# Attention's value and memory products on the full 128x128 array, and other prices in the list schedule

## The chip, the cores and the metric

The kernel runs as one program on one core of a Trainium2 chip. TensorE (PE) does the matmuls, VectorE (DVE) and ScalarE (ACT) the elementwise work, GpSimd (POOL) a few memsets, and SyncE (SP) issues all the DMAs. The metric is the device time of one execution in microseconds; lower is better.

## The reference

Attention with a memory, and then two feed-forward layers over the tokens that it gives:

```python
B, H, S, D = 4, 8, 576, 64            # batches, heads, tokens, head width
scores = q @ k.T / sqrt(D)            # causal
local = softmax(scores) @ v
q_p = phi(q)                          # phi(x) = max(x, 0) + min(exp(x), 1)
mem_out = (q_p @ M_prev) / (q_p @ z_prev + 1e-6)
x = g * mem_out + (1 - g) * local     # g = sigmoid(beta), by head
# 2304 tokens, d_model 512, d_ff 2048
h = x @ w_in;   x = (s * relu(h) ** 2 + b) @ w_out
h = x @ w_in2;  out = (max(h, 0) + alpha * min(h, 0)) @ w_out2
```

## The kernel before, in words

Attention works head by head, and the memory part by pair of heads. A head's 576 queries stand in five chunks of 64, 128, 128, 128 and 128, and a chunk sees the keys up to its last query, so 64, 192, 320, 448 and 576 of them. Chunks 0 to 2 are set 0, chunks 3 and 4 are set 1; a set's results gather in one PSUM bank. For each chunk `scores` makes the scores in one of the banks for scores (`sp`, two of them after the first batch) and their exponentials, `turn` splits the normalised weights in two float16 parts and transposes them by a DMA (L564), and `products` (L584) multiplies them with the values, 128 keys at a time, into the bank `ob`. Every chunk's number of keys ends in half a block: the last product of each chunk reads 64 keys, so 64 rows of the array.

`features` (L454, L463) computes the memory part of a pair with queries on the partitions. `remembered` (L598) turns it with a matmul against the identity into the bank `ob`, on top of what the products give. Batches 0 and 1 do this by pair (`pair`, with float32 scores, L627). Batches 2 and 3 do it head by head (`head`, with float32r scores, L673 and L674): each head turns its own 64 columns, and then ACT (L695) takes one half of the bank's rows and DVE (L697) adds the other half. The array's tile is as large as the operands: 64 key rows give a tile of 64 rows, 64 output rows one of 64 columns. The profile writes it as 64\*128 (rows \* columns).

The feed-forward layers (called MoE in the code) run over blocks of tokens, and over 16 slices of d_ff in each: 12 matmuls for the first product (L800 to L802) and 12 for the second (L834 to L836) a slice. Layer 1 has blocks of 512, 320 and 320 tokens and then four of 288, layer 2 eight of 288. Blocks 0 to 2 lie in batches 0 and 1, blocks 3 and 4 in batch 2, blocks 5 and 6 in batch 3 (block 0 needs only batch 0). A batch's attention goes to DRAM (`x1`, L719) and a block is read from it (L890).

The order on every engine is fixed when the program is built. `Plan.order` is a list schedule: each operation has a duration and a priority, attention's coming before the layers', and an engine takes the most urgent of what its own clock says is ready. On the chip an engine then keeps that order and waits on semaphores. So prices such as `t_r` (a float32r matmul) and the rate of a DMA (transposes are those with a `dur` of 500 or more) decide the order alone:

```python
dma_free = max(dma_free + (110.0 if dur < 500 else 30.0), t + min(dur, 625.0) + 650.0) + nbytes / (360.0 if dur < 500 else 290.0)
def t_r(n):
    return max(108.0, n / 2.4 + 2.5)
```

Of the kernel before, what the change touches and what calls it, by code (L numbers as in the profile page):

```python
# [18 lines left out]
# tokens of the blocks of the two layers: (first, tokens); layer 1's first takes both places of the operands  # L19
# [6 lines left out]
# query chunks: (first query, queries); a chunk sees the keys up to its last query  # L26
CHUNKS = [(0, 64), (64, 128), (192, 128), (320, 128), (448, 128)]
SETS = [(0, 1, 2), (3, 4)]
# chunks whose weights are transposed together
# [16 lines left out]
FLEX = 'x'  # L46
# [7 lines left out]
class Slot:  # L54
    """A tenant of the pool of equal slots; it gets its place when the operations are ordered."""
# [6 lines left out]
class Plan:  # L62
    """Operations in a logical order with what they read and write. order() is a list schedule
    of the graph: every engine takes, of the operations that are ready, the most urgent. A slot
    is taken by its first operation, if as many more are free as the slot's reserve asks, and
    is free again after its last."""
# [38 lines left out]
    def either(self, ways, **kw):  # L105
        """An operation for whichever of the engines comes to it first: ways is {engine: (duration, function)}."""
        eng = next(iter(ways))
        i = self.op(eng, *ways[eng], **kw)
        if len(ways) > 1:
            self.ways[i] = ways  # L110

    def order(self):
# [32 lines left out]
        def spot(t, s):  # L145
            """Where a slot could go: the last extra place, or else the one that has been free for longest."""
# [12 lines left out]
        while len(out) < n:  # L159
# [50 lines left out]
            if e == "PE":  # L210
                # at half the clock unless the last tick was busy enough
                todo, now, k = dur, t, int(t / TICK)
                while todo > 0:
                    rate = 1.0 if busy.get(k - 1, 0.0) >= WARM else 0.5
                    step = min(todo, max(0.0, (k + 1) * TICK - now) * rate)
                    busy[k] = busy.get(k, 0.0) + step
                    todo -= step
                    now += step / rate
                    k += 1
                dur = now - t  # L220
            free[e] = t + dur
            done[i] = t + dur
            if nbytes:
                dma_free = max(dma_free + (110.0 if dur < 500 else 30.0), t + min(dur, 625.0) + 650.0) + nbytes / (360.0 if dur < 500 else 290.0)
# [25 lines left out]
def t_r(n):  # L250
    return max(108.0, n / 2.4 + 2.5)
# [18 lines left out]
def build(tc, kd, kz, qd, vd, qp, mzd, beta8, sb2, win1, wout1, win2, wout2, alpha, outT):  # L270
# [7 lines left out]
    with tc.tile_pool(name="sb", bufs=1) as sb, tc.tile_pool(  # L278
# [5 lines left out]
        # the parts of a slice of d_ff: w_in's and w_out's; before they are there, the last slices' room serves as slots  # L284
# [13 lines left out]
        def cut(t, n, k, step=None):  # L298
            """The first n elements of the k-th part of t."""
# [28 lines left out]
        def at(s, n, dt=F32):  # L328
            """The first n elements of a slot, as dt."""
# [12 lines left out]
        # the last 128 columns: -8e9 where the key lies after the query  # L342
# [7 lines left out]
        def consts():  # L350
            # wsc = (1 + exp(beta)) / LIFT = 1 / ((1 - g) LIFT); bgc = 1 + exp(-beta) = 1 / g
# [16 lines left out]
        # the banks of MoE products serve the first batch's attention  # L368
# [8 lines left out]
        def gate(hg, ahead, ahead0):  # L377
            """A load for a head waits for the scores of an earlier one."""
# [3 lines left out]
        def either(kind, a_dur, a_fn, d_dur, d_fn, **kw):  # L382
            """An operation for the scalar or, of the kinds in FLEX, also for the vector engine."""
# [10 lines left out]
        # They are scaled by LIFT over the sum of their magnitudes, so that no part leaves float16's range.  # L394
        def values(b, p):
# [19 lines left out]
            # un = 1 / (scale LIFT)  # L415
# [53 lines left out]
        def scores(b, h, g, keys, scored):  # L469
            """keys: what the products read; scored: (rows, columns) -> the product's instructions."""  # L470
# [4 lines left out]
            for c in cs:  # L475
# [4 lines left out]
                # keys in one or two banks: (bank, column of maximum and sum, first key, keys)  # L480
# [10 lines left out]
                for bk, col, k0, kn in parts_s:  # L491
                    sp = bank_of[bk][0:nq, 0:kn]
                    dur, mm = scored(sp, q0, nq, k0, kn)
# [20 lines left out]
            # rows 64.. of chunk 0's column were set once and stay finite  # L514
# [8 lines left out]
        def turn(b, g, group, parts, turned):  # L523
            """group: what is transposed together, (head of the pair, chunk)."""
# [13 lines left out]
            for pw, c in group:  # L538
# [19 lines left out]
                # what is transposed with the chunk's last 64 keys has to be something; nothing uses it  # L558
# [8 lines left out]
        def products(g, part, parts, turned, sf, obk, ok, high, rows, first=False):  # L567
            """The products with the values: part (head of the pair, chunk) into rows of the bank. high: the high and
            low parts of the values go to the same rows, else the low ones follow in the next 64."""
# [6 lines left out]
            def mm():  # L576
                P = p_t()
                W = at(sf, 2 * NKB * 2 * D, FP16).rearrange("p (n h e) -> p n h e", h=2, e=2 * D)
                for kb in range(nkb):
                    kk = min(128, nk - kb * 128)  # L580
                    cols = [(slice(0, D), kb), (slice(D, 2 * D), kb), (slice(0, D), nkb + kb)] if high else [
                        (slice(0, 2 * D), kb), (slice(0, 2 * D), nkb + kb)]
                    for w, x in cols:
                        T.matmul(obk[rows, q0 - o0:q0 - o0 + nq], W[0:kk, kb, pw, w], P[0:kk, x, 0:nq],  # L584
# [4 lines left out]
        def remembered(g, heads, sa, obk, ok, rows, ch, first=True):  # L589
            """The memory part, transposed into the bank."""  # L590
# [3 lines left out]
            def mm():  # L594
                for c in cs:
                    q0, nq = CHUNKS[c]
                    F = at(sa, 2 * D * NC).rearrange("p (c e) -> p c e", c=NC)[0:nq, c, heads]
                    T.matmul(obk[rows, q0 - o0:q0 - o0 + nq], F, ident[0:nq, 0:nq], start=(first and c == cs[0]), stop=False,  # L598
                             skip_group_check=True)

            op("PE", sum(t_f(CHUNKS[c][1]) for c in cs), mm, r=[(sa, g), "ident"], w=[ok], prio=ATT + ch * 10)
# [7 lines left out]
        def pair(b, p, sqp, sa, sf, xt):  # L609
# [9 lines left out]
            for g, cs in enumerate(SETS):  # L619
# [4 lines left out]
                for odd in range(2):  # L624
                    def scored(sp, q0, nq, k0, kn, s=sk[odd]):
                        def mm():
                            T.matmul(sp, at(sqp, S)[:, q0:q0 + nq], at(s, S)[:, k0:k0 + kn], start=True, stop=True)  # L627
# [10 lines left out]
                remembered(g, slice(0, 2 * D), sa, obk, ok, slice(0, 128), ch0)  # L638
# [8 lines left out]
                # local + memory, transposed  # L647
# [7 lines left out]
        def head(b, h, sa, sf, xt):  # L655
# [15 lines left out]
            def scored(sp, q0, nq, k0, kn):  # L671
                def mm():
                    T.matmul(sp, qh[:, q0:q0 + nq], ks[:, k0:k0 + kn], start=True, stop=False)  # L673
                    T.matmul(sp, ql[:, q0:q0 + nq], ks[:, k0:k0 + kn], start=False, stop=True)  # L674
# [3 lines left out]
            for g, cs in enumerate(SETS):  # L678
# [9 lines left out]
                remembered(g, slice(D * odd, D * odd + D), sa, obk, ok, slice(r0, r0 + 64), ch0, False)  # L688
# [5 lines left out]
                # local + memory, transposed  # L694
                op("ACT", t_act(qn, 50, 93), lambda xr=xr, qn=qn, obk=obk: A.activation(  # L695
# [305 lines left out]
```

## Time and profile before

| | us |
|---|---|
| three runs | 1095.52, 1096.52, 1099.56 (median 1096.52) |
| profiled execution: its time (the listed one that fits the span) and its span | 1099.56, 1099.4 |
| PE busy | 1073.4, 98% of the span |
| DVE, ACT busy | 684.6 (62%), 529.8 (48%) |
| attention's last store of a batch to DRAM, batches 1, 2, 3 | issued at 246.71, 412.96, 568.99 |
| first feed-forward matmul | 104.85 |

Busy time of PE counts a matmul from start to end, and matmuls overlap in the pipeline. What a matmul costs is therefore read as the distance from its start to the start of the next, which the timeline gives.

### The profile page before, as it was taken

To read this page: it belongs to the slowest core of one execution; us is meant where nothing else is said; L and a number is where in the kernel's file an instruction comes from. 1 tells how busy PE (TensorE), PEld (TensorE's weight loads), DVE (VectorE), ACT (ScalarE), POOL (GpSimd) and SP (SyncE) were. 2 spreads that over 40 slices of the span, in tenths; PEclk is the share of its full clock that TensorE was granted. 3 is DMA by queue.
4 is the path that set the end of the run, shared out by engine and by line. 5 is a ranking of instruction groups with operands and counts; after the bars stand their busy time and mean duration, and the time that the engine had idled before them with its cause. 6 is when DMAs were issued, how large, how long until landed. Compare 5 with 4: busy or idle time off the path is not lost.

```text
span 1099.4 us, 20528 instructions
## 1 busy us (share of the span) xinstructions
PE 1073.4 (98%) x7776; PEld 976.4 (89%) x7776; DVE 684.6 (62%) x1812; ACT 529.8 (48%) x1325; POOL 32.2 (3%) x171
## 2 busy tenths in 40 slices
PE   7978999999999999999999999999999999999998
PEld 5755777777889989989999999999999999999998
DVE  6768888867575566566646179984545454545443
ACT  7764666558576667668654466331212121212111
POOL 1100000000000000000000000000000000000000
PEclk9987999999999999999999999999999999999999
DMA  8899686665644564454434055321101010100000
GB/s 211 162 182 259 203 182 192 181 141 167 134 72 125 132 135 109 118 125 106 96 105 154 1 185 193 129 73 32 44 1 44 1 44 1 44 1 22 1 22 23
DMA packets 163860, 114.10 MB, mean 104 GB/s; under 512 B 127408, under 2 KB 141744, under 8 KB 163760
## 3 DMA queue, kind: packets, MB, share of 16 engines
q1 hardware_dynamic: 163760, 112.78, 39.1%
q8 instruction: 61, 1.00, 0.4%
q14 instruction: 39, 0.32, 0.1%
HBM read 68.19 MB, written 14.16 MB: 75 GB/s over the span
## 4 chain that ended last, share of the span: by engine, by line
PE 88%; DMA 5%; DVE 2%; issue 2%; ACT 2%; SPq 0%; POOL 0%; DVEq 0%; POOLq 0%; ACTq 0%
PE yb L834 12%; PE yb L836 12%; PE yb L835 12%; PE hb L800 8%; PE hb L802 7%; PE hb L801 7%; PE ob L584 7%; PE sp L800 3%; PE sp L801 3%; PE sp L802 3%; PE ob L598 2%; PE sp L627 2%; DMA pool<-pool 2%; PE ob L802 2%; PE ob L800 2%
## 5 line engine op out<-in xcount | busy, mean ns | idle before, releaser
L834 PE MATMUL yb<-gr,wt 128*128 128x288 f32 (+3 forms) x960 | 299.0, 311 | 0.9 <-ACT gr L822 0.9
L835 PE MATMUL yb<-gr,wt 128*128 128x288 f32 (+3 forms) x960 | 291.7, 304 | 0.0
L836 PE MATMUL yb<-gr,wt 128*128 128x288 f32 (+3 forms) x960 | 291.6, 304 | 0.0
L822 ACT CAST gr<-gt 128x288 fp32r<-128x288 f32 (+2 forms) x240 | 107.4, 447 | 305.4 <-DVE gt L820 297.0
L823 DVE TENSOR_TENSOR gr<-gt,gr 128x288 fp32r<-128x288 f32 (+2 forms) x240 | 114.2, 476 | 139.1 <-ACT gr L822 138.6
L800 PE MATMUL hb<-xr,wt 128*128 128x288 f32 (+2 forms) x576 | 186.1, 323 | 1.7 <-ACT gt L814 1.7
L834 PEld LDWEIGHTS yb<-gr,wt 128*128 128x128 f32 x960 | 181.0, 189 | 7.6 <-issue 2.1
L836 PEld LDWEIGHTS yb<-gr,wt 128*128 128x128 f32 x960 | 181.3, 189 | 3.6 <-DVE gr L823 0.8
L835 PEld LDWEIGHTS yb<-gr,wt 128*128 128x128 f32 x960 | 180.9, 188 | 2.0 <-issue 0.2
L802 PE MATMUL hb<-xr,wt 128*128 128x288 f32 (+2 forms) x576 | 178.6, 310 | 0.0
L801 PE MATMUL hb<-xr,wt 128*128 128x288 f32 (+2 forms) x576 | 178.6, 310 | 0.0
L800 PEld LDWEIGHTS hb<-xr,wt 128*128 128x128 f32 x576 | 108.8, 189 | 8.6 <-ACT gt L814 2.6
L801 PEld LDWEIGHTS hb<-xr,wt 128*128 128x128 f32 x576 | 109.0, 189 | 2.9 <-issue 0.6
L802 PEld LDWEIGHTS hb<-xr,wt 128*128 128x128 f32 x576 | 108.9, 189 | 3.0
L814 ACT ACTIVATE gt<-hb 128x288 f32<-128x288 f32 (+2 forms) x112 | 49.7, 444 | 106.8 <-PE hb L802 105.8
L505 ACT ACTIVATE pool<-sp,mx 64x64 f32<-64x64 f32 (+2 forms) x153 | 72.4, 474 | 35.4 <-DVE mx L497 27.2
L584 PEld LDWEIGHTS <-pool 64*64 64x64 f16 (+3 forms) x930 | 55.1, 103 | 38.1 <-issue 19.7
L497 DVE CUSTOM_DVE_ANT_0 sp<-sp,mask 64x64 f32<-64x64 f32 (+4 forms) x132 | 56.5, 438 | 42.6 <-PE sp L674 26.5
L584 PE MATMUL ob<-pool 128*128 128x128 f16 (+5 forms) x855 | 76.8, 221 | 4.1 <-DMA pool<-pool 4.0
L800 PE MATMUL sp<-xr,wt 128*128 128x288 f32 x256 | 75.5, 295 | 0.0
L801 PE MATMUL sp<-xr,wt 128*128 128x288 f32 x256 | 75.5, 295 | 0.0
L802 PE MATMUL sp<-xr,wt 128*128 128x288 f32 x256 | 75.4, 295 | 0.0
(174 smaller groups left out, 1694.1 us busy)
## 6 DMA issues: line engine op xcount, KB each, us to landing
pool<-win SPq DMA_DIRECT2D x19, 512.0 KB, 4.4
pool<-wout SPq DMA_DIRECT2D x17, 512.0 KB, 4.5
room<-wout SPq DMA_DIRECT2D x15, 512.0 KB, 4.3
room<-win SPq DMA_DIRECT2D x13, 512.0 KB, 4.3
pool<-qd SPq DMA_DIRECT2D x16, 288.0 KB, 3.1
pool<-kd SPq DMA_DIRECT2D x16, 288.0 KB, 3.7
pool<-y SPq DMA_DIRECT2D x16, 288.0 KB, 3.4
out_t<-pool SPq DMA_DIRECT2D x32, 144.0 KB, 1.8
```

The source lines that it names most:

```text
L497: op("DVE", t_dve(kn, 1.04, 0 if mk is None else 60), lambda sp=sp, nq=nq, mo=mo, kn=kn, mcol=mcol, last=last: V.tensor_tensor_reduce(out= ...
L505: op("ACT", t_act(kn, 50, 180), lambda sp=sp, p_c=p_c, k0=k0, kn=kn, mcol=mcol, scol=scol: A.activation(out=p_c()[:, k0:k0 + kn], in_=sp, ...
L584: T.matmul(obk[rows, q0 - o0:q0 - o0 + nq], W[0:kk, kb, pw, w], P[0:kk, x, 0:nq], start=(first and kb == x == 0), stop=False, skip_group_c ...
L800: T.matmul(H_, W_h, X_h, start=(d == 0), stop=False)
L801: T.matmul(H_, W_h, X_l, start=False, stop=False)
L802: T.matmul(H_, W_l, X_h, start=False, stop=(d == KD - 1))
L814: op("ACT", t_act(n, 50), lambda: A.activation(out=t_, in_=H_, func=AF.Relu), r=[hk, "gr"], w=[tk], prio=-1)
L822: op("ACT", t_act(n), lambda: A.copy(out=G_h, in_=t_), r=[tk], w=[("gh", gj)], prio=-1)
L823: op("DVE", t_dve(n), lambda: V.tensor_tensor(out=G_l, in0=t_, in1=G_h.bitcast(F32), op=ALU.subtract), r=[tk, ("gh", gj)], w=[("gl", gj)], ...
L834: T.matmul(Y, W_h, G_h, start=(f == 0), stop=False)
L835: T.matmul(Y, W_l, G_h, start=False, stop=False)
L836: T.matmul(Y, W_h, G_l, start=False, stop=(f == KF - 1))
```

## The change

In batches 2 and 3 the memory part is turned once a pair (`recall`, new) in a score bank, all 128 columns at a time, and ACT or DVE writes it scaled to the output slot before the heads come. `head` no longer calls `remembered`; DVE adds both halves of its bank to the slot, one after the other, and ACT does none. In all batches `products` reads 128 rows of weights and values (the weights behind a chunk's last key were set to zero by POOL before the transpose), and the scores of chunk 0 and the turned memory part use 128 columns of the array; rows that nobody asked for are not read. Float32r matmuls, transposes and loads have other prices in the schedule. Comments are left out of the new file, and line numbers move: L673/L674 become L687/L688, L697 becomes L709, L800 to L802 L813 to L815, L834 to L836 L847 to L849; L584 and L598 stay.

```diff
-                dma_free = max(dma_free + (110.0 if dur < 500 else 30.0), t + min(dur, 625.0) + 650.0) + nbytes / (360.0 if dur < 500 else 290.0)
+                dma_free = max(dma_free + (110.0 if dur < 500 else 30.0), t + min(dur, 625.0) + 650.0) + nbytes / (330.0 if dur < 500 else 160.0)
...
 def t_r(n):
-    return max(108.0, n / 2.4 + 2.5)
+    return max(112.0, n * 0.4427 + 3.2)
...
                 for kb in range(nkb):
-                    kk = min(128, nk - kb * 128)
...
-                        T.matmul(obk[rows, q0 - o0:q0 - o0 + nq], W[0:kk, kb, pw, w], P[0:kk, x, 0:nq],
+                        T.matmul(obk[rows, q0 - o0:q0 - o0 + nq], W[:, kb, pw, w], P[:, x, 0:nq],
                                  start=(first and kb == x == 0), stop=False, skip_group_check=True)
...
-        def remembered(g, heads, sa, obk, ok, rows, ch, first=True):
+        def remembered(g, sa, obk, ok, prio):
...
-                    F = at(sa, 2 * D * NC).rearrange("p (c e) -> p c e", c=NC)[0:nq, c, heads]
-                    T.matmul(obk[rows, q0 - o0:q0 - o0 + nq], F, ident[0:nq, 0:nq], start=(first and c == cs[0]), stop=False,
+                    F = at(sa, 2 * D * NC).rearrange("p (c e) -> p c e", c=NC)[:, c]
+                    T.matmul(obk[:, q0 - o0:q0 - o0 + nq], F, ident[:, 0:nq], start=(c == cs[0]), stop=False,
                              skip_group_check=True)
...
+        def recall(b, p, sa, xt):
+
+            j = p % 2
+            for g in range(len(SETS)):
+                ok = next_bank(b, "S")
+                obk = bank_of[ok]
+                remembered(g, sa, obk, ok, ATT + cnt["ch"] * 10 - 4)
+                o0, qn = span_of(g)
+                either("x", t_act(qn, 50, 93), lambda o0=o0, qn=qn, obk=obk: A.activation(
+                    out=at(xt, S)[:, o0:o0 + qn], in_=obk[:, 0:qn], func=AF.Copy, scale=vsc[:, j, 1:2]),
...
+                    r=[ok, ("un", j)], w=[(xt, odd, g) for odd in range(2)])
...
-                    T.matmul(sp, qh[:, q0:q0 + nq], ks[:, k0:k0 + kn], start=True, stop=False)
-                    T.matmul(sp, ql[:, q0:q0 + nq], ks[:, k0:k0 + kn], start=False, stop=True)
+                    T.matmul(sp, qh[:, q0:q0 + 128], ks[:, k0:k0 + kn], start=True, stop=False)
+                    T.matmul(sp, ql[:, q0:q0 + 128], ks[:, k0:k0 + kn], start=False, stop=True)
...
-                remembered(g, slice(D * odd, D * odd + D), sa, obk, ok, slice(r0, r0 + 64), ch0, False)
...
-                op("ACT", t_act(qn, 50, 93), lambda xr=xr, qn=qn, obk=obk: A.activation(
-                    out=xr(), in_=obk[r1:r1 + 64, 0:qn], func=AF.Copy, scale=un[r0:r0 + 64]), r=[ok, ("un", j)], w=[(xt, odd, g)])
-                op("DVE", t_dve(qn, 1.04, 60), lambda xr=xr, qn=qn, obk=obk: V.scalar_tensor_tensor(
-                    out=xr(), in0=obk[r0:r0 + 64, 0:qn], scalar=un[r0:r0 + 64], in1=xr(),
-                    op0=ALU.mult, op1=ALU.add), r=[("un", j)], w=[ok, (xt, odd, g)])
+                for r, w in ((r1, []), (r0, [ok])):
+                    op("DVE", t_dve(qn, 1.04, 60), lambda xr=xr, qn=qn, obk=obk, r=r: V.scalar_tensor_tensor(
+                        out=xr(), in0=obk[r:r + 64, 0:qn], scalar=un[r0:r0 + 64], in1=xr(),
+                        op0=ALU.mult, op1=ALU.add), r=[ok, ("un", j)], w=w + [(xt, odd, g)])
...
-                    head(b, 2 * p, sa, sf, xt)
-                    head(b, 2 * p + 1, sa, sf, xt)
+                    recall(b, p, sa, xt)
+                    head(b, 2 * p, sf, xt)
+                    head(b, 2 * p + 1, sf, xt)
```

The order on PE before, in batch 2 at the end of the set 0 of a head: products, the memory part of this head (output 64 rows), then feed-forward matmuls.

```order
L584 MATMUL ob<-pool 128x128
L598 MATMUL ob<-ident,pool 64x64
L598 MATMUL ob<-ident,pool 64x128 x2
L834 MATMUL yb_93<-gr,wt_1750 128x322
L835 MATMUL yb_93<-gr,wt_1750 128x322
```

The same memory part in the changed kernel, now for both heads of the pair, in a score bank and between feed-forward matmuls:

```order
L815 MATMUL hb<-xr,wt_1825 128x320
L598 MATMUL sp_98<-ident,pool 128x64
L598 MATMUL sp_98<-ident,pool 128x128 x2
L813 MATMUL hb<-xr,wt_1825 128x320
L814 MATMUL hb<-xr,wt_1825 128x320
```

It has left the end of each head's set, stands once a pair before the heads' products, and its tile has 128 columns. In the whole program the array's tile changes its size 469 times from one matmul to the next before, 345 of them after the first feed-forward matmul and 233 after the first score of batch 2; in the changed kernel 108, 64 and 0 times.

The second place is where PE turns to the feed-forward layers for the first time. Before, score and product matmuls of batch 1 stand ahead of it:

```order
L627 MATMUL sp_98<-pool 128x288
L584 LDWEIGHTS pool
L584 MATMUL ob<-pool 64x64
L584 LDWEIGHTS pool
L584 MATMUL ob<-pool 64x64
L800 MATMUL hb<-xr,wt_885 128x512
L801 MATMUL hb<-xr,wt_885 128x512
```

In the changed kernel:

```order
L627 MATMUL sp_98<-pool 128x320
L627 MATMUL sp_99<-pool 128x192
L813 MATMUL hb<-xr,wt_982 128x512
L814 MATMUL hb<-xr,wt_982 128x512
L815 MATMUL hb<-xr,wt_982 128x512
L627 MATMUL sp_99<-pool 128x64
L627 MATMUL sp_98<-pool 128x192
```

The first 21 products of batch 1 and 8 of its score matmuls now come behind the first feed-forward matmul; 464 matmuls stand ahead of it in place of 493. From there on the two orders mix alike: when the last product of batch 1 stands, 342 feed-forward matmuls are ahead of it before and 357 after, and at the last product of batch 3 1791 and 1782.

## Rows read from the trace of the kernel before

**Rows 1.** Page, busy time by engine; granted clock of PE in 40 slices

```profile
PE 1073.4 (98%) x7776; PEld 976.4 (89%) x7776; DVE 684.6 (62%) x1812; ACT 529.8 (48%) x1325; POOL 32.2 (3%) x171
PEclk9987999999999999999999999999999999999999
```

**Rows 2.** Stages: length, then busy PE, PEld, DVE, ACT, POOL; clock, DMA share, GB/s

```profile
0.00:105.00 105.00, 87.67 (x606) 60.31 (x606) 78.88 (x296) 73.32 (x207) 10.15 (x59) 0.91 0.88 202
105.00:247.00 142.00, 141.80 (x829) 105.16 (x830) 113.59 (x301) 85.95 (x201) 7.29 (x32) 0.98 0.70 182
247.00:413.00 166.00, 163.17 (x1173) 145.15 (x1172) 106.77 (x321) 117.80 (x302) 7.58 (x41) 1.00 0.53 127
413.00:569.00 156.00, 155.31 (x1212) 141.44 (x1211) 94.95 (x286) 107.71 (x287) 7.19 (x39) 1.00 0.44 104
695.00:1099.00 404.00, 400.46 (x3022) 399.80 (x3021) 212.86 (x457) 77.08 (x177) 0.00 (x0) 1.00 0.09 31
```

**Rows 3.** Page, chain that ended last, by engine

```profile
PE 88%; DMA 5%; DVE 2%; issue 2%; ACT 2%; SPq 0%; POOL 0%; DVEq 0%; POOLq 0%; ACTq 0%
```

**Rows 4.** Timeline of PE, one head of batch 2: start, us, matmuls

```profile
403.14 1.03 PE L584 MATMUL ob<-pool 128*128 128x128 f16 x10
404.11 0.91 PE L598 MATMUL ob<-ident,pool 64*64 64x64 f32 x6
404.94 0.41 PE L800 MATMUL hb<-xr,wt 128*128 128x320 f32 x1
405.19 0.31 PE L801 MATMUL hb<-xr,wt 128*128 128x320 f32 x1
...
408.61 0.72 PE L584 MATMUL ob<-pool 128*128 128x128 f16 x8
409.26 0.42 PE L800 MATMUL hb<-xr,wt 128*128 128x320 f32 x1
409.51 0.31 PE L801 MATMUL hb<-xr,wt 128*128 128x320 f32 x1
...
410.26 0.84 PE L584 MATMUL ob<-pool 128*128 128x128 f16 x10
411.02 0.65 PE L598 MATMUL ob<-ident,pool 128*64 128x128 f32 x4
411.61 0.41 PE L834 MATMUL yb<-gr,wt 128*128 128x320 f32 x1
411.86 0.31 PE L835 MATMUL yb<-gr,wt 128*128 128x320 f32 x1
```

**Rows 5.** Timeline of PE: float32 matmuls on the full tile, then feed-forward

```profile
324.17 1.28 PE L454 MATMUL sp<-mz,pool 128*128 128x130 f32 x10
325.20 0.39 PE L800 MATMUL hb<-xr,wt 128*128 128x320 f32 x1
325.43 0.31 PE L801 MATMUL hb<-xr,wt 128*128 128x320 f32 x1
325.57 0.31 PE L802 MATMUL hb<-xr,wt 128*128 128x320 f32 x1
```

**Rows 6.** Waits between 280 and 570 us: total, times, longest

```profile
DVE sp L497 <- PE sp L674: 29.0, 38, 2.3
ACT pool L695 <- PE ob L598: 21.1, 22, 2.7
```

**Rows 7.** Groups between 280 and 569 us: busy, mean ns | idle before

```profile
L584 PE MATMUL ob<-pool 128*128 128x128 f16 x308 | 27.7, 221 | 1.4 <-DMA pool<-pool 1.4
L697 DVE SCALAR_TENSOR_TENSOR pool<-ob,vsc,pool 64x256 f32<-64x256 f32 (+1 forms) x31 | 15.9, 514 | 16.4 <-ACT pool L695 16.1
```

**Rows 8.** Timeline: batch 3's last store and the loads of block 5; its second product

```profile
568.99 0.33 SPq L719 DMA_DIRECT2D x<-pool  x1
...
573.53 1.20 SPq L890 DMA_DIRECT2D pool<-x  x2
...
588.25 0.30 PE L834 MATMUL yb<-gr,wt 128*128 128x288 f32 x1
```

More of the change, by code (lines that the diff above doesn't have):

```diff
@@ L491, in scores @@
                 for bk, col, k0, kn in parts_s:
+                    dur, mm = scored(bank_of[bk][:, 0:kn], q0, k0, kn)
                     sp = bank_of[bk][0:nq, 0:kn]
-                    dur, mm = scored(sp, q0, nq, k0, kn)
                     op("PE", dur, mm, r=keys, w=[bk] + ([("hs", b * H + h)] if c == NC - 1 else []), prio=ATT + ch * 10)
@@ L596, in mm @@
                     q0, nq = CHUNKS[c]
-                    F = at(sa, 2 * D * NC).rearrange("p (c e) -> p c e", c=NC)[0:nq, c, heads]
-                    T.matmul(obk[rows, q0 - o0:q0 - o0 + nq], F, ident[0:nq, 0:nq], start=(first and c == cs[0]), stop=False,
+                    F = at(sa, 2 * D * NC).rearrange("p (c e) -> p c e", c=NC)[:, c]
+                    T.matmul(obk[:, q0 - o0:q0 - o0 + nq], F, ident[:, 0:nq], start=(c == cs[0]), stop=False,
                              skip_group_check=True)
-            op("PE", sum(t_f(CHUNKS[c][1]) for c in cs), mm, r=[(sa, g), "ident"], w=[ok], prio=ATT + ch * 10)
+            op("PE", sum(t_f(CHUNKS[c][1]) for c in cs), mm, r=[(sa, g), "ident"], w=[ok], prio=prio)
         def span_of(g):
@@ L624, in pair, with scored @@
                 for odd in range(2):
-                    def scored(sp, q0, nq, k0, kn, s=sk[odd]):
+                    def scored(sp, q0, k0, kn, s=sk[odd]):
                         def mm():
-                            T.matmul(sp, at(sqp, S)[:, q0:q0 + nq], at(s, S)[:, k0:k0 + kn], start=True, stop=True)
+                            T.matmul(sp, at(sqp, S)[:, q0:q0 + 128], at(s, S)[:, k0:k0 + kn], start=True, stop=True)
                         return t_f(kn), mm
@@ L637, in pair @@
                             turn(b, g, [(odd, c) for c in group], parts, turned)
-                remembered(g, slice(0, 2 * D), sa, obk, ok, slice(0, 128), ch0)
+                remembered(g, sa, obk, ok, ATT + ch0 * 10)
                 for odd in range(2):
@@ L652, in pair, with head @@
                     r=[ok, ("un", j)], w=[(xt, odd, g) for odd in range(2)])
-        def head(b, h, sa, sf, xt):
+        def recall(b, p, sa, xt):
[7 more added lines that the diff above has]
+                    out=at(xt, S)[:, o0:o0 + qn], in_=obk[:, 0:qn], func=AF.Copy, scale=vsc[:, j, 1:2]),
+                    t_dve(qn, 1.04, 60), lambda o0=o0, qn=qn, obk=obk: V.tensor_scalar(
+                    out=at(xt, S)[:, o0:o0 + qn], in0=obk[:, 0:qn], scalar1=vsc[:, j, 1:2], scalar2=None, op0=ALU.mult),
+                    r=[ok, ("un", j)], w=[(xt, odd, g) for odd in range(2)])
+        def head(b, h, sf, xt):
             hg = b * H + h
@@ L669, in head, with scored @@
                 out=ql, in0=at(sq, S), in1=qh.bitcast(F32), op=ALU.subtract), r=[sq, "qh"], w=["ql"])
-            def scored(sp, q0, nq, k0, kn):
+            def scored(sp, q0, k0, kn):
                 def mm():
-                    T.matmul(sp, qh[:, q0:q0 + nq], ks[:, k0:k0 + kn], start=True, stop=False)
-                    T.matmul(sp, ql[:, q0:q0 + nq], ks[:, k0:k0 + kn], start=False, stop=True)
+                    T.matmul(sp, qh[:, q0:q0 + 128], ks[:, k0:k0 + kn], start=True, stop=False)
+                    T.matmul(sp, ql[:, q0:q0 + 128], ks[:, k0:k0 + kn], start=False, stop=True)
                 return 2 * t_r(kn), mm
```

## The prediction

> **What bounds the kernel now.** I read the busy times first, then the stages, then the chain, and last the timeline of PE in one head. PE is busy 98% of the span, no other engine over 62% [rows 1]. The stages show that this isn't the same everywhere [rows 2]. Up to 105 us, in batch 0's attention, PE has 87.67 us of 105, the DMA engines 88%, and the clock is granted at 0.91; PE isn't the limit there. From 105 to 569 us PE has practically all of each stage (141.80 of 142, 163.17 of 166, 155.31 of 156) while DVE has 61% to 80% of it and ACT 61% to 71%. From 695 us on there is only layer 2, which the change doesn't touch. The chain agrees: 88% of it is PE, 5% DMA [rows 3]. So time that PE no longer needs between 105 and 569 us comes off the end, as long as the next matmul in its fixed order is ready.
>
> A busy PE is not a working PE, though, and the timeline of a head shows what attention's matmuls cost it [rows 4]. The eight products of chunk 3 (six on 128 rows, two on 64) take 409.26 - 408.61 = 0.65 us, the ten of chunk 4 (eight and two) 411.02 - 410.26 = 0.76. Two full ones are 0.11, one is 0.055. The two half ones with the way into their tile and out of it are therefore 0.65 - 6 x 0.055 = 0.32, where two full ones would be 0.11. The run of chunks 1 and 2, with six full matmuls and a half block in each chunk, confirms it: 6 x 0.055 + 2 x 0.32 = 0.97, and 404.11 - 403.14 is 0.97. A half block costs 0.21 us that it need not. The same holds for the turned memory part on half the columns: four float32 passes take 0.59 (411.02 to 411.61) and the matmul behind them comes 0.25 later, where 0.14 is normal [rows 4, 5]. Ten float32 passes on the full tile with the matmul behind them take 325.43 - 324.17 = 1.26, so 1.12 without that matmul, 0.112 a pass, and nothing at the way out [rows 5].
>
> **The change, part by part.** Products and memory part of a head of batches 2 and 3, before [rows 4]: chunks 1 and 2 0.97, memory 0.83, way out 0.25 - 0.14 = 0.11; chunk 3 0.65, way out 0.11; chunk 4 0.76, memory 0.59, way out 0.11; in all 4.13 us. After: 28 full products x 0.055 = 1.54; half of a pair's ten passes x 0.112 = 0.56; and three ways out from a float16 run on the full tile into a feed-forward matmul. No run before ends so; at most they cost what they cost now (0.33), at least nothing. That is 2.10 to 2.43, a gain of 1.70 to 2.03, for which I take the middle, 1.87. Sixteen heads give 27.2 to 32.5, **taken as 29.9 us**.
>
> Against this rule and row stand apart in one point. A half block uses 64 rows of the array, and the row of chunk 3 shows that its two matmuls cost more than full ones [rows 4]. The Trainium skill, page TensorEngine Tiling (Array Packing), section Performance Considerations, advises row tiling for a contraction of up to 64, since tiles may work at the same time. By that rule the full tile would give up a gain; by the row there is no gain to give up, since the half block takes 0.32 and not under 0.11.
>
> Chunk 0: its two products are a half block of their own and gain up to 0.21 a head, 3.4 in all. Its two score matmuls load 128 columns in place of 64; a float32 pass with its load is 0.112 [rows 5], so they cost 0 to 0.22 a head more, up to 3.6. I set both against each other, **0** (-3.4 to +3.6). On loads the Trainium skill, TensorE: Matmul & The Clock Gate, section LDWEIGHTS, says that a load takes the columns over 1.2 GHz; estimated from it, 64 more columns are 53 ns, 1.7 us over the 32 matmuls, and the sum would be 1.7 less.
>
> Batch 1 (105 to 247 us) loses 112 - 64 = 48 changes of tile, of 0.105 each (half of 0.21), 5.0 us. But DVE is at 80% there, the highest of all stages on this side [rows 2], and PE runs short of feed-forward work when batch 1 ends, as block 1 needs it. I take half, **2.5** (0 to 5).
>
> Evacuation: 32 operations leave ACT and come to DVE at 0.514 us [rows 7], 16.5 us, and 16 new full-width ones go to either. DVE has 106.77 + 94.95 = 201.7 of 322 us in these two stages; with 218 in some 292 it is at 75%. ACT goes the other way. Cover is there: **0**. Without it, with DVE the limit, those 16.5 us would come back. A new set's products need the bank and wait for the second addition; before, they waited for PE's memory passes, ACT and DVE in turn.
>
> The score banks get two more tenants a pair. The prices change only the order; the two orders mix feed-forward and attention alike, and the transposes' dearer price puts products later, if it does anything. PE's wait for transposed data is small already, 1.4 us in 289 [rows 7]. **0**, with 4 us either way. For the stage up to 105 us I take nothing either: DMA sets it and moves the same bytes; the first feed-forward matmul has 29 fewer matmuls ahead of it, of which any gain of some us is within that bound.
>
> What comes late next: attention must now go through in less time. A pair takes about 322/8 = 40 us and would take 36. DVE, ACT and DMAs must deliver a tenth sooner, and small stalls will show; I take **+2** (0 to 8).
>
> Sum: -29.9 - 2.5 + 2 = -30.4. The profiled execution took 1099.56, so 1069.2; it lies 3.0 above the median of the runs, which makes 1066.2. **I predict 1066**, and 1054 to 1078 if this case holds.
>
> **The rivals.** *Attention keeps its pace.* If what paces a pair is its chain of scores, exponentials, transposes and loads, PE gets ahead with the feed-forward blocks and then waits for batch 3. Its last store is issued at 568.99, its block 5 is loaded by issues from 573.53 on; the block's second product starts at 588.25, and its first, 12 matmuls of 404/3022 = 0.134 sooner, at 586.7 [rows 2, 8]. Of the 13 us between issue and start I take half as needed for landing and for the split of the operands. So some 7 us are gained and no more: 1090. For it: those 7 us are all the room there is, and the forecast wants 30 by then. Against it: in these stages DVE waits for score matmuls (29.0 us in 38 waits) and ACT for the memory passes (21.1 us in 22) [rows 6], so attention waits for PE and will move with it.
>
> *The tile isn't the price.* If the 0.21 comes from the change of operands and weights within a run and not from the tile, only the passes go: 8 pairs x 10 x 0.112 = 9 us, 1087. Against it: within a run nothing else changes but the rows.
>
> *Slower: the memory part blocks the score banks.* `recall` stands early on PE, behind the matmuls that it depends on through DVE (L463). PE keeps its order; if DVE hasn't written the part, PE stands still with the scores and the feed-forward work queued behind, and the bank is held until ACT or DVE has read it. The gain is 30.4 us over 8 pairs, 3.8 a pair; 1.9 us for each of the two turns use it up, and 2.2 each (4.5 a pair) make the kernel 0.5% slower, about 1102. For it: ACT, which empties the bank most often, is at 69% to 71% [rows 2]. Against it: the order leaves feed-forward matmuls between the memory part and the turn.
>
> *Half tiles do work side by side.* If the two matmuls of a half block could share the array, as one full matmul's time, they would take 0.055 where the changed kernel takes 0.11. Eight pairs have 80 half blocks in five chunks a head, a loss of 80 x 0.055 = 4.4 us against the 9 us of the halved passes: 1096.5 - 4.6 = 1092, which can't be told from no change. Against it stands the 0.32 of a half block. It is what row tiling on that page of the Trainium skill would do here.
>
> **How the numbers follow.** Two results of this kernel tell apart from about 0.5%, 5.5 us. Chances: the forecast 0.72; attention's pace 0.11; not the tile 0.06; score banks 0.05; half tiles side by side 0.02; more gained at the start or at the ways out than I bound 0.04. Leaving out 0.02 below and the tail above 1089 (half of attention's pace, the score banks, the half tiles side by side) the range is 1053 to 1089. Faster: 0.72 + 0.04 + 0.06 and half of 0.11, so 0.88 (1090 lies near the bound of 1091); same 0.07; slower 0.05.
>
> **What will show it.** Right: no half-tile forms in batches 2 and 3; a run of ten products taking 0.55 to 0.6; half as many L598 passes there, 0.112 each; batch 3's last store some 30 us earlier; stages still full on PE. Wrong: the stores of batches 2 and 3 at their old places and PE idle ahead of blocks 3 and 5; the first feed-forward matmul moved by more than 4 us; PE waiting at L598; DVE over 85%.

## The result, and the profile after

The changed kernel takes 1071.23 us (median of four runs, 1070.67 to 1072.59) against 1097.54 (1095.52 to 1099.56): ratio 0.9756, 95% interval 0.9736 to 0.9776, 26 us faster. Forecast were 1066 in a range of 1053 to 1089. The two profiled executions differ by 1099.4 - 1069.7 = 29.7 us, the sum of the prediction was 30.4.

From the page of the changed kernel, the busy times and the clock granted in 40 slices:

```profile
PE 1028.9 (96%) x7696; PEld 966.1 (90%) x7696; DVE 703.6 (66%) x1851; ACT 518.0 (48%) x1302; POOL 31.7 (3%) x171
PEclk9986999999999999999999999999999999999999
```

Its stages, with columns as in [rows 2]; the third ends with batch 2's last store, the fourth with batch 3's:

```profile
0.00:105.00 105.00, 74.82 (x571) 57.77 (x571) 77.12 (x276) 67.54 (x184) 9.36 (x54) 0.87 0.81 209
105.00:247.00 142.00, 139.60 (x854) 106.36 (x855) 118.78 (x326) 92.09 (x221) 7.46 (x37) 1.00 0.71 176
247.00:397.00 150.00, 148.38 (x1148) 140.89 (x1147) 113.55 (x335) 111.40 (x292) 8.08 (x43) 1.00 0.59 141
397.00:539.00 142.00, 140.34 (x1162) 136.37 (x1161) 103.34 (x306) 101.83 (x276) 6.82 (x37) 1.00 0.49 114
663.00:1069.00 406.00, 402.78 (x3040) 402.12 (x3038) 213.98 (x457) 77.21 (x176) 0.00 (x0) 1.00 0.09 30
```

The last stores of batches 2 and 3 were issued at 396.92 and 538.81, 16 and 30 us sooner than before (batch 1's at 249.86, 3 us later), with PE as full as in [rows 2]. PE lost 13 us of work up to 105 us, and the clock there fell from 0.91 to 0.87. The first feed-forward matmul starts at 103.51 (before 104.85), block 1's second product at 263.69 (265.69), block 5's at 558.61 (588.25, [rows 8]). So of 29.7 us, 1.3 come up to the first feed-forward matmul, 0.7 more up to block 1, 27.7 from there to block 5 (batches 2 and 3), and none later.

The timeline of PE in a head of batch 2, which answers to [rows 4]:

```profile
381.24 0.62 PE L584 MATMUL ob<-pool 128*128 128x128 f16 x8
381.67 0.39 PE L813 MATMUL hb<-xr,wt 128*128 128x320 f32 x1
381.90 0.31 PE L814 MATMUL hb<-xr,wt 128*128 128x320 f32 x1
382.05 0.31 PE L815 MATMUL hb<-xr,wt 128*128 128x320 f32 x1
...
388.99 0.83 PE L598 MATMUL sp<-ident,pool 128*128 128x64 f32 x6
389.58 0.40 PE L813 MATMUL hb<-xr,wt 128*128 128x320 f32 x1
389.82 0.30 PE L814 MATMUL hb<-xr,wt 128*128 128x320 f32 x1
...
390.11 0.73 PE L584 MATMUL ob<-pool 128*128 128x128 f16 x10
390.65 0.39 PE L847 MATMUL yb<-gr,wt 128*128 128x320 f32 x1
...
391.63 0.61 PE L598 MATMUL sp<-ident,pool 128*128 128x128 f32 x4
392.00 0.39 PE L847 MATMUL yb<-gr,wt 128*128 128x320 f32 x1
392.23 0.31 PE L848 MATMUL yb<-gr,wt 128*128 128x320 f32 x1
```

Eight products take 381.67 - 381.24 = 0.43 us where they took 0.65, ten 0.54 where they took 0.76 or 0.97. Behind a run of products the second feed-forward matmul still comes 0.23 behind the first in place of 0.15, 0.08 more. The runs themselves are 0.01 shorter than 8 and 10 x 0.055, so the way out keeps about 0.07. The ten passes of a pair take 0.69 and 0.46 with the way out (389.82 - 388.99 and 392.23 - 391.63, less 0.14).

Added up over all matmuls between block 1's and block 5's second product, as distances from start to start in the two traces (a distance over 0.4 us counts as a wait for what exceeds it):

| us | before | after |
|---|---|---|
| feed-forward | 222.7 | 223.3 |
| products L584 | 40.7 | 25.6 |
| memory passes L598 | 22.7 | 7.3 |
| scores | 26.2 | 28.5 |
| features, value sums | 9.1 | 8.4 |
| waits | 1.1 | 1.8 |

The memory passes in the stretch are 160 before and 70 after, in place of 80, since the changed kernel makes the ten of batch 2's first pair ahead of block 1.

Where the start went wrong shows on PE between 82 and 104 us (in brackets the idle time ahead and what ended it):

```profile
82.11 0.91 PE L454 MATMUL sp<-mz,pool 128*128 128x130 f32 x6 [0.61 <-ACT room L648]
94.15 0.58 PE L413 MATMUL sp<-vsc,allone 128*128 128x1 f32 x2 [11.13 <-ACT pool L411]
97.19 1.23 PE L454 MATMUL sp<-mz,pool 128*128 128x130 f32 x4 [2.45 <-DVE vsc L416]
100.18 0.69 PE L627 MATMUL sp<-pool 128*128 128x64 f32 x2 [1.76 <-DVE pool L463]
100.66 1.59 PE L598 MATMUL ob<-ident,pool 128*128 128x64 f32 x6
102.05 1.91 PE L627 MATMUL sp<-pool 128*128 128x320 f32 x4
103.51 0.87 PE L813 MATMUL hb<-xr,wt 128*128 128x512 f32 x1
```

The value sum of batch 1's first pair (L413) keeps PE waiting for 11.13 us, and the features and scores behind it for 4 more. Batch 0's last store was issued at 86.0, 5.6 us sooner than before; nothing of this was used.

### The profile page after: what moved, and what is told of

Read it like the earlier page. It is cut to its first block, busy times and chain, and to the rows that moved or that the text cites. A ratio compares the mean times of both kernels' runs of the same rounds, so it can differ in the third digit from the quotient of the medians.

```text
span 1069.7 us, 20374 instructions
## 1 busy us (share of the span) xinstructions
PE 1028.9 (96%) x7696; PEld 966.1 (90%) x7696; DVE 703.6 (66%) x1851; ACT 518.0 (48%) x1302; POOL 31.7 (3%) x171
## 4 chain that ended last, share of the span: by engine, by line
PE 86%; DMA 4%; DVE 4%; issue 2%; ACT 2%; SPq 1%; POOL 0%; DVEq 0%; ACTq 0%; POOLq 0%
PE yb L847 12%; PE yb L849 12%; PE yb L848 12%; PE hb L813 8%; PE hb L815 7%; PE hb L814 7%; PE ob L584 5%; PE sp L813 3%; PE sp L814 3%; PE sp L815 3%; DMA pool<-pool 3%; PE sp L627 2%; PE ob L815 2%; PE ob L813 2%; PE ob L814 2%
## 5 line engine op out<-in xcount | busy, mean ns | idle before, releaser
L847 PE MATMUL yb<-gr,wt 128*128 128x288 f32 (+3 forms) x960 | 298.4, 311 | 0.6 <-ACT gr L835 0.5
L849 PE MATMUL yb<-gr,wt 128*128 128x288 f32 (+3 forms) x960 | 291.6, 304 | 0.0
L836 DVE TENSOR_TENSOR gr<-gt,gr 128x288 fp32r<-128x288 f32 (+2 forms) x240 | 114.4, 477 | 128.8 <-ACT gr L835 127.6
L813 PE MATMUL hb<-xr,wt 128*128 128x288 f32 (+2 forms) x576 | 187.6, 326 | 2.0 <-ACT gt L827 2.0
L847 PEld LDWEIGHTS yb<-gr,wt 128*128 128x128 f32 x960 | 181.2, 189 | 4.1 <-ACT gr L835 1.3
L849 PEld LDWEIGHTS yb<-gr,wt 128*128 128x128 f32 x960 | 181.3, 189 | 3.5 <-DVE gr L836 0.6
L815 PE MATMUL hb<-xr,wt 128*128 128x288 f32 (+2 forms) x576 | 177.9, 309 | 0.0
L813 PEld LDWEIGHTS hb<-xr,wt 128*128 128x128 f32 x576 | 108.7, 189 | 6.7 <-ACT gt L827 3.2
L815 PEld LDWEIGHTS hb<-xr,wt 128*128 128x128 f32 x576 | 108.5, 188 | 2.9
L506 ACT ACTIVATE pool<-sp,mx 64x64 f32<-64x64 f32 (+2 forms) x156 | 73.9, 475 | 37.2 <-DVE mx L498 27.7
L556 DVE SCALAR_TENSOR_TENSOR pool<-pool,sm 128x192 f16<-128x192 f32 (+4 forms) x137 | 72.5, 545 | 10.0 <-ACT pool L552 8.9
L552 ACT ACTIVATE pool<-pool,sm 128x192 f16<-128x192 f32 (+4 forms) x137 | 70.8, 555 | 12.2 <-DVE sm L520 3.6
L813 PE MATMUL sp<-xr,wt 128*128 128x288 f32 x256 | 75.5, 295 | 0.0
L815 PE MATMUL sp<-xr,wt 128*128 128x288 f32 x256 | 75.4, 295 | 0.0
L584 PEld LDWEIGHTS <-pool 128*128 128x128 f16 (+1 forms) x930 | 53.5, 104 | 21.9 <-issue 14.9
## 6 DMA issues: line engine op xcount, KB each, us to landing
pool<-qd SPq DMA_DIRECT2D x16, 288.0 KB, 3.3
pool<-kd SPq DMA_DIRECT2D x16, 288.0 KB, 3.5
pool<-y SPq DMA_DIRECT2D x16, 288.0 KB, 3.3
```

Source lines behind the costliest of these rows:

```text
L506: op("ACT", t_act(kn, 50, 180), lambda sp=sp, p_c=p_c, k0=k0, kn=kn, mcol=mcol, scol=scol: A.activation(out=p_c()[:, k0:k0 + kn], in_=sp, ...
L552: either("p", t_act(nk, 93, 93), lambda w_c=w_c, p_c=p_c, sc=sc, nk=nk: A.activation(out=w_c()[:, 0:nk], in_=p_c(), func=AF.Copy, scale=sc ...
L556: op("DVE", t_dve(nk, 1.04, 60), lambda w_c=w_c, p_c=p_c, sc=sc, nk=nk, nkb=nkb: V.scalar_tensor_tensor(out=w_c()[:, 128 * nkb:128 * nkb + ...
L584: T.matmul(obk[rows, q0 - o0:q0 - o0 + nq], W[:, kb, pw, w], P[:, x, 0:nq], start=(first and kb == x == 0), stop=False, skip_group_check=True)
L813: T.matmul(H_, W_h, X_h, start=(d == 0), stop=False)
L815: T.matmul(H_, W_l, X_h, start=False, stop=(d == KD - 1))
```

## The experiments

All ratios are to the kernel before on the same chip. "Block 1" is the start of its second product in the profiled execution.

| kernel | median us | ratio, interval | block 1 |
|---|---|---|---|
| changed | 1071.2 | 0.9756 (0.9736 to 0.9776) | 263.7 |
| e1_rows | 1080.2 | 0.9837 (0.9813 to 0.9862) | 254.9 |
| e2_prices | 1108.7 | 1.0099 (1.0068 to 1.0130) | 278.2 |
| e3_body | 1064.8 | 0.9693 (0.9679 to 0.9708) | 253.0 |
| e4_recall | 1086.4 | 0.9890 (0.9875 to 0.9905) | 261.7 |
| e5_tr | 1063.5 | 0.9678 (0.9644 to 0.9713) | 254.9 |
| e6_turns | 1074.4 | 0.9776 (0.9745 to 0.9808) | 271.0 |
| e7_loads | 1066.0 | 0.9701 (0.9673 to 0.9728) | 256.7 |
| e8_less | 1064.8 | 0.9683 (0.9652 to 0.9714) | 260.3 |
| e9_mix | 1054.9 | 0.9610 (0.9587 to 0.9633) | 252.3 |
| e10_early | 1073.2 | 0.9777 (0.9753 to 0.9800) | 264.1 |
| e11_dear0 | 1066.9 | 0.9729 (0.9705 to 0.9753) | 256.7 |
| e12_dear1 | 1065.6 | 0.9723 (0.9694 to 0.9752) | 259.9 |

**The parts of the change by themselves.** e1 on the kernel before:

```diff
-                    kk = min(128, nk - kb * 128)
...
-                        T.matmul(obk[rows, q0 - o0:q0 - o0 + nq], W[0:kk, kb, pw, w], P[0:kk, x, 0:nq],
+                        T.matmul(obk[rows, q0 - o0:q0 - o0 + nq], W[:, kb, pw, w], P[:, x, 0:nq],
```

> The kernel before with one edit: the products read 128 rows in place of 64 in each chunk's last half block; the order on every engine is that of before, instruction for instruction. Theory (each half block costs PE 0.21 us for the way into its tile and out, and PE sets the time from 105 us on): 80 half blocks in batches 2 and 3 give 16.8 us, the 40 of batch 1 some 4 more, so 17 to 21 us off, ratio 0.981 to 0.985. Rival (attention keeps its pace): 7 us at most. Rival (the tile isn't the price): within 2 us.

Measured: 18 us off, with the same order. The tile is the price. From block 1 to block 5, the products by their tile, of the kernel before (two lines) and of e1, where they stand on L583 (chunk 0's 32 are left out):

```profile
L584 PE MATMUL ob<-pool 128*128 128x128 f16 x320 | 28.9, 221 | 1.4 <-DMA pool<-pool 1.4
L584 PE MATMUL ob<-pool 64*128 64x128 f16 x128 | 18.1, 221 | 0.0
```

```profile
L583 PE MATMUL ob<-pool 128*128 128x128 f16 x448 | 33.3, 220 | 3.5 <-DMA pool<-pool 3.5
```

In this stretch the trace gives 11.1 us and not 16.8 (322.6 to 311.4): 2.2 us are new waits, and 3.0 are the 32 ways from a run into the memory part, which still has half the columns (0.149 us in e1's trace in place of 0.056). Another 10.8 us came ahead of block 1, where the theory had some 4.

e2 is the kernel before with the changed prices, e3 the changed kernel without them, e4 is e3 with the half blocks back.

> The kernel before with the new prices alone (float32r matmuls and DMAs in the schedule). Theory (prices only move the order, and the early stage up to the first feed-forward matmul is a little worse for it): 0 to 4 us slower or faster, ratio 0.997 to 1.004. Rival (the better prices are what made the kernel faster): 10 us or more off.

> The changed kernel with the old prices. Theory: the whole gain of the body, 26 to 32 us off, ratio 0.971 to 0.976, and no wait of 11 us of PE near 83 us, since the old prices give the early order of before. Rival (prices carry a good part of the gain): less than 20 us off.

> As e3_body, but the products read 64 rows in half blocks as before; the order is that of e3_body, instruction for instruction. What is left is the memory part once a pair on the full tile, the other evacuation and chunk 0's scores on 128 columns. Theory: 9 us for the halved passes and some 8 for their tile (0.25 and 0.27 a set of a head), so 13 to 18 us off, ratio 0.984 to 0.988, and 12 to 20 us more than e3_body. Rival (the tile isn't the price): equal to e3_body.

Measured: e3 gains 34 us, a little over its theory, and its first feed-forward matmul starts at 98.2. e4 gains 12, just short of its bound, and e3 and e4 differ by 21.6, a little over the 20: once more the half blocks. e2 went against the theory: the prices alone cost 10 us, all of it ahead of block 1, which starts 12.5 later. With the changed body they cost 6.5 (1071.2 to 1064.8).

That loss is what is left of a loss and a gain. Block 1 starts at 253.0 in e3 and 10.7 us later in the changed kernel, but from there to block 5 e3 takes 297.9 us and the changed kernel 294.9, since PE waits longer for transposed weights in e3. The products of this stretch, of e3 and of the changed kernel (busy, mean | idle ahead of them):

```profile
L584 PE MATMUL ob<-pool 128*128 128x128 f16 (+1 forms) x480 | 36.5, 218 | 7.7 <-DMA pool<-pool 6.8 <-DVE sm L520 0.8
```

```profile
L584 PE MATMUL ob<-pool 128*128 128x128 f16 (+1 forms) x480 | 37.0, 218 | 1.3 <-DMA pool<-pool 1.3
```

**Which price.** e5 to e7 are the changed kernel with one of the three new prices each:

```diff
 e5_tr:    t_r new, nbytes / (360.0 if dur < 500 else 290.0)
 e6_turns: t_r old, nbytes / (360.0 if dur < 500 else 160.0)
 e7_loads: t_r old, nbytes / (330.0 if dur < 500 else 290.0)
```

> The changed kernel, of the new prices only the float32r matmul's. Theory (the transposes' price is what costs time, in the stage up to the first feed-forward matmul and in batch 1; the matmul's price helps batches 2 and 3 by about 3 us): first feed-forward matmul near 98 us, time 1060 to 1066. Rival (the matmul's price costs the time): 1070 or more.

> The changed kernel, of the new prices only that of the DMA transposes (loads and matmuls at the old ones). Theory: it carries the loss; first feed-forward matmul near 103 us, PE idle for some 10 us or more between 80 and 100, time 1070 to 1076. Rival (another price): as e3_body, 1065.

> The changed kernel, of the new prices only that of loads and stores (330 in place of 360). Theory: it does next to nothing, 1063 to 1067, first feed-forward matmul near 98 us. Rival (this price carries the loss): 1070 or more.

Measured: the transposes' price carries the loss (1074.4), the others none. e5's first feed-forward matmul came at 100.5 and e7's at 103.5, later than expected, though e7 lost nothing by it. The 3 us that e5 was to gain in batches 2 and 3 by the matmul's price didn't come: from block 1 to block 5 it takes 299.5 us, e3 297.9, e7 295.2 and e6, with the dear transposes, 290.7.

**Where dear transposes help and where they hurt.** e9 is e5 with the dear price for the transposes of batches 2 and 3 (`EXACT` is batches 0 and 1; the durations 1240 and 1241 only tell the two prices apart). Its edit is shown against the changed kernel, with lines cut at `...`:

```diff
-... nbytes / (330.0 if dur < 500 else 160.0)
+... nbytes / (360.0 if dur < 500 else 290.0 if dur == 1240 else 160.0)
...
-            op("SP", 1240, lambda: nc.sync.dma_start_transpose(...
+            op("SP", 1240 if b in EXACT else 1241, lambda: nc.sync.dma_start_transpose(...
```

> The changed kernel with the new matmul price, the old price of loads, and the dear transposes in batches 2 and 3 alone (old price in batches 0 and 1). Theory (dear transposes spoil the order of batches 0 and 1 and keep PE from waits in batches 2 and 3): block 1 starts near 254 us as in e5_tr, then 295 us to block 5 as in the changed kernel, PE waits after 265 us near 2 us, time 1056 to 1062, the fastest so far. Rival (the gain of batches 2 and 3 isn't the transposes' price): as e5_tr, 1063 or more.

Measured: 1054.9, the fastest of all, just under its range and 16 us under the changed kernel. Groups of products between block 1 and block 5 (busy, mean | idle ahead of them), of e5 and of e9:

```profile
L584 PE MATMUL ob<-pool 128*128 128x128 f16 (+1 forms) x480 | 37.4, 220 | 6.7 <-DMA pool<-pool 6.3 <-DVE ql L682 0.4
```

```profile
L584 PE MATMUL ob<-pool 128*128 128x128 f16 (+1 forms) x480 | 37.0, 219 | 0.3 <-DMA pool<-pool 0.2
```

With transposes priced dearly the products stand late enough that PE is idle for 0.3 us ahead of them and not 6.7; that stretch takes 289.9 us in e9 and 299.5 in e5. The changed kernel, with the same price there, takes 294.9, so the price isn't all that sets these waits.

e10 is the changed kernel with this for the loads of batch 1's first pair, shown for the values and done alike for queries and keys (lines cut at `...`):

```diff
-            sv, sf = Slot(RES["v"], early), ...
+            sv, sf = Slot(3 if (b, p) == (1, 0) else RES["v"], early), ...
...
-               ... prio=-7 if b + p == 0 else None, ...
+               ... prio=-7 if b + p == 0 else -5 if (b, p) == (1, 0) else None, ...
```

> The changed kernel with all its prices, but the loads of batch 1's first pair get an earlier priority and a smaller reserve of slots, so that SP issues its values behind 19 transposes in place of 32 and its keys behind 26 and 27 in place of 32; the mix of batches 2 and 3 stays as it was. Theory (these loads, put behind all of batch 0's transposes, are what PE waits for between 83 and 94 us): that wait goes, first feed-forward matmul at 97 to 101 us, 3 to 8 us off the changed kernel, 1063 to 1068. Rival (the early loss lies elsewhere, as in the order of DVE and ACT): 1070 to 1073.

Measured: the 11 us wait went and the first feed-forward matmul came at 97.6, both as the theory has it, and the time didn't move, as the rival has it. Block 1 started at 264.1, because PE now waited later, in batch 1, for the transposes ahead of its products, 5.4 us in four waits; the longest is 3.80:

```profile
240.45 1.02 PE L584 MATMUL ob<-pool 128*64 128x128 f16 x15 [0.29 <-DMA pool<-pool]
245.28 0.83 PE L584 MATMUL ob<-pool 128*64 128x128 f16 x12 [3.80 <-DMA pool<-pool]
```

e11 and e12 then put the dear transposes back into one of the two first batches: in the edit of e9, `b == 1` (e11) or `b == 0` (e12) in place of `b in EXACT`.

> e9_mix with the dear transposes in batch 0 as well (so in batches 0, 2 and 3, the old price in batch 1 alone). Theory A (the order of batch 0's end is what is lost: loads and scores of batch 1 late, PE and DVE empty between 80 and 100 us): block 1 near 262 in place of 252, time 1062 to 1066. Theory B (the price of batch 1's transposes does it, since the schedule then spends feed-forward matmuls of block 0 too early: 264 in place of 204 ahead of product 600): as e9_mix, 1054 to 1057.

> e9_mix with the dear transposes in batch 1 as well (the old price in batch 0 alone). Theory A: as e9_mix, 1054 to 1057. Theory B: block 1 near 262, PE waits of several us for transposes near the end of batch 1, 1062 to 1066.

Measured: both lose 11 to 12 us, so each theory names a part. Block 1 starts 4.4 us later with batch 0 dear and 7.6 with batch 1 dear; the sum, 12.0, is close to the 11.4 of the changed kernel with both. That isn't the whole loss, though. From block 1 to block 5, where their price is that of e9, e11 takes 6.5 us more than e9 and e12 2.1. In e11 PE waits there for transposed weights again:

```profile
L584 PE MATMUL ob<-pool 128*128 128x128 f16 (+1 forms) x480 | 36.9, 218 | 5.3 <-DMA pool<-pool 5.1
```

Why the same price serves these batches less well behind another start is not shown. Ahead of block 1, in e11 PE is busy for 13.90 us between 80 and 100 at a clock of 0.60; in e9 for 16.65 at 0.81:

```profile
80.00:100.00 20.00, 13.90 (x70) 10.08 (x68) 12.70 (x42) 9.28 (x25) 1.10 (x6) 0.60 0.78 263
```

```profile
80.00:100.00 20.00, 16.65 (x102) 11.06 (x101) 17.39 (x57) 12.34 (x35) 0.87 (x5) 0.81 1.02 284
```

In e12 the first feed-forward matmul comes as early as 96.6, and PE stands still at the end of batch 1 instead. The waits of PE from 98 to 262 us in e12 (total, times, longest), and one stretch:

```profile
PE hb L813 <- ACT wt L774: 3.6, 1, 3.6
PE hb L815 <- DVE wt L777: 2.5, 1, 2.5
```

```profile
220.00:240.00 20.00, 14.25 (x108) 10.25 (x106) 8.96 (x21) 6.84 (x15) 0.41 (x2) 0.93 0.78 182
```

The waits aren't for transposes, as theory B had them, but for the last weights of layer 1 (L774, L777): block 0's matmuls were used early, 264 in place of 204 ahead of product 600, and then came before their weights were converted.

The number of feed-forward matmuls ahead of product 600 (the 600th L584 matmul, in batch 1) goes with the loss in all kernels with the whole changed body. From the first feed-forward matmul to block 1 they take 153 to 155 us where 204 to 240 stand there (e3, e5, e7, e9, e11), 160 at 255 (the changed kernel, e8), 163 at 264 (e12), and 166.5 and 168.5 at 309 and 300 (e10, e6). With the body of before it is 161 at 228 (the kernel before) and 166 at 255 (e2). So e10 won 5.9 us at its start and lost 6.3 behind it. The 10.7 us between e3 and the changed kernel are 5.3 up to the first feed-forward matmul and 5.4 from there to block 1.

**Does PE still set the pace of batches 2 and 3?** e8, with the order of the changed kernel, leaves out the products with the weights' low-order part in these batches:

```diff
-                        (slice(0, 2 * D), kb), (slice(0, 2 * D), nkb + kb)]
+                        (slice(0, 2 * D), kb)]
```

> The changed kernel with the same order on every engine, but in batches 2 and 3 the products with the low-order part of the weights are left out (half of the L584 matmuls there: 14 full ones and a short one a head). Theory (PE sets the pace of these batches): 15 x 0.055 = 0.8 us a head, 13 us over 16 heads, ratio to the changed kernel 0.987 to 0.990, about 1058. Rival (attention has now reached its own pace, and PE would only wait): 4 us at most, 1067 to 1072.

Measured: between the two. From block 1 to block 5 the trace gives 294.9 - 288.0 = 6.9 us, of the 11.9 that the products take less. The rest came back, 1.8 in longer feed-forward distances, 0.9 in scores, 1.0 in waits over 0.4 us, 1.2 in memory passes, features and value sums. The other 3.4 us of difference between the profiles lie ahead of block 1, where no matmul was left out: by so much the early stage varies from execution to execution, and the 4.4 and 7.6 above must be read with that.

## Why the prediction was right

**Half blocks and memory part (29.9 us, less 2 for attention's pace).** Shown, and well sized. In the table products and memory passes take 30.5 us less, or 29.4 when the ten passes that are made ahead of block 1 are counted too. What arrives depends on PE's waits: from block 1 to block 5 the body alone gives 24.7 us (e3), the changed kernel 27.7, against 27.9 forecast. So 3 of the 27.7 come from the prices. A head's products and its half of the memory part now take 0.43 + 2 x 0.54 + 3 x 0.08 + 0.57 = 2.3 us, forecast 2.10 to 2.43. The ways out, bounded between nothing and 0.33, are about 0.2 (three of 0.07). e1 and the pair e3, e4 show that the size of the tile is what cost the half blocks; for the memory part no run parts the tile from the number of passes. The Trainium skill, TensorEngine Tiling (Array Packing), section Key Properties, says that a change of tiling mode drains the array; the traces fit this, at about 0.1 us a change, though they don't show the drain itself. The Trainium skill's advice for short contractions (the same page, section Performance Considerations), held against the change in the prediction, doesn't pay here, where half blocks stand among full ones: e1 gave up the half tiles and gained 18 us.

**Chunk 0 (nothing).** The scores cost 2.3 us more in the table, though 95 pairs of score matmuls fall in the stretch after and 91 before; four pairs more are some 1.2 of it. The bound of 3.6 was kept.

**Attention's pace (2 us).** The stages stayed full and DVE came to 73% to 76%, as worked out. Waits and scores took 0.7 and 2.3 us more. With the old prices the waits alone take 5.5 more (e3, 6.6 in place of 1.1), over the 2 but within the 8. e8 shows that little margin is left: of further PE work some two fifths come back as longer distances and waits.

**The stage to 105 us and batch 1 (0 and 2.5).** 1.3 and 0.7 were measured, but the reason was wrong. By e3 the body gives 6.7 and 6.0 there (first feed-forward matmul at 98.2, block 1 at 253.0), so "DMA sets it and moves the same bytes" fell: with the same bytes and the early order of before, the full tiles brought the first feed-forward matmul sooner, by 4.3 us in e1 and by 6.0 from e4 to e3, against the 3.0 by which it differs between e8 and the changed kernel.

**The prices ("change only the order ... 0, with 4 us either way").** This step failed: they cost 6.5 us with the body and 10 without. "29 fewer matmuls ahead" of the first feed-forward matmul was read as a possible gain; in this order PE stood waiting for some 15 us between 83 and 101, for the values, features and scores of batch 1's first pair, and then used block 0's matmuls too early. That dearer transposes put products later did come true, in batches 2 and 3, and gave 3 us there. Up to block 1 the two misses, 10.2 us of body too little (12.7 in place of 2.5) and 10.7 of prices too little, nearly cancelled. That was luck, and it is why the total is nearer to the mark than its parts.

**The shift to the median.** 3 us were taken off because the profiled execution was the slowest listed. The changed kernel's runs, 1070.67 to 1072.59, spread about the 1071.48 of its profiled execution, and 26.3 us lie between the medians where the two profiles differ by 29.7. With before at 1097.54 the sum of 30.4 gives 1067.

The rivals: the tile is the price (e1, e4); the score banks brought no wait of note, 0.2 us at L598; half tiles didn't work side by side; attention's own pace wasn't reached, but is near. What stays open is which operations of batch 0 and 1 a dear transpose displaces first; e10 shows that the loads of batch 1's first pair alone aren't it. That matmuls used early cost the time behind the first one is seen in e12's waits and in the row of counts above; no run changes that count alone.

## What to carry to other kernels

Where one engine is full, price its short operations by the distance from start to start, with the ways into and out of a run: here a half-filled block cost three times the full one. A list schedule's prices are part of the kernel: change them alone, stage by stage, before they go in together with a body. And a price nearer to the chip isn't better by that: the new float32r price gives 0.145 us for 320 columns, the old one 0.136, the trace shows 0.147, and alone it left the time where it was (e5 against e3). One price need not fit all stages either: dear transposes cost 11.4 us ahead of block 1 (the changed kernel against e9), and behind it gained 9.6 in e9 against e5, 7.2 in e6 against e3, but only 0.3 in the changed kernel against e7.

## What the hardware showed that was not expected

Behind a run on the full tile, float16 or float32, the first float32r matmul of 320 columns comes 0.03 us behind the run's last matmul and the second 0.23 behind the first, where 0.15 is normal (medians of 11 and 6 places between block 1 and block 5 of the changed kernel). Together that is 0.26. Behind a float32 run it is what a pass and a float32r matmul take anyhow, 0.112 + 0.147; behind a float16 run it is 0.055 more than 0.056 + 0.147. So a float16 run keeps a small way out even on the full tile, and a float32 run none. Behind a half block of 128 queries it was 0.15 + 0.25 = 0.40 (6 places before), so about 0.14 of that was the tile.

In PE's empty stretch of the changed kernel, 80 to 100 us, the clock was granted at 0.67 in the mean with PE busy for 4.17 us of 20. In shorter windows it was 1.00 from 82 to 86 us, 0.65 from 86 to 90 (PE had been idle since 83), and 0.50, the level of 1.2 GHz, from 90 to 104. PE was busy for 1.82 and 2.00 of each 2 us from 100 to 104, and from 104 to 106 the clock was 0.94. So all matmuls from the end of the wait at 94.15 to the first feed-forward one ran at the lower level:

```profile
80.00:100.00 20.00, 4.17 (x32) 3.32 (x29) 12.54 (x28) 6.28 (x11) 0.71 (x3) 0.67 0.88 331
```
